# A new issue order for a hand-scheduled RG-LRU and gated-unit kernel, with one output copy on another engine

## The chip, the core and the metric

The kernel runs on one core of one Trainium2 chip. The core has five engines that run their own instruction streams: TensorE (PE in the profile, with its weight loads as PEld), VectorE (DVE), ScalarE (ACT), GpSimd (POOL) and SyncE (SP), which here issues nearly all DMA transfers. Each engine executes its instructions in the order in which they are issued; an instruction whose input isn't ready, or whose output buffer isn't free, holds all that stand behind it on that engine. The metric is device time in microseconds, median of several runs.

## What is computed

A gated linear recurrence over 6336 steps for 4 sequences of width 256, and on its output a gated linear unit whose gate is a causal convolution of 5 taps:

```python
a_base = 1.0 / (1.0 + np.exp(-a_param))
sig_r = 1.0 / (1.0 + np.exp(-r_gate))
sig_i = 1.0 / (1.0 + np.exp(-i_gate))
log_a = c * sig_r * np.log(np.clip(a_base, 1e-06, 1.0 - 1e-06))[None, None, :]
a_t = np.exp(log_a)
norm = np.sqrt(np.maximum(1.0 - a_t * a_t, 1e-06))
x_gated = norm * sig_i * x
for t in range(S):
    h = a_t[:, t] * h + x_gated[:, t]
    y[:, t] = h
...
for k in range(K):
    gate_pre += conv_w[k][None, None, :] * xp[:, k:k + S, :]
gate = 1.0 / (1.0 + np.exp(-gate_pre))
val = x @ w_val
return (gate * val @ w_out).astype(np.float32)
```

In the second half `x` is the `y` of the first. Inputs x, r_gate, i_gate and the output are float32 arrays of 26 MB each, so some 104 MB pass between memory and core.

## The kernel before

The 25344 rows (4 x 6336) are cut into 51 windows of 512 rows (the first two and the last have 256). A chunk (28 of them, line 17) is one or two windows; most work on a chunk of 1024 rows at once. Rows arrive with time along the partitions, as they lie in memory; the recurrence needs channels along the partitions and time along the free axis, so data is transposed on TensorE. The 256 channels are two halves, h = 0 and 1.

There are no loops that set the order. The text ORDER (line 38) is a list of 976 words, and lines 557 to 563 go through it and issue each word's operation. A word is a name, its indices, and behind @ the PSUM banks (of eight) that TensorE writes. Each engine's stream is what is left of the list when the other engines' words are taken out. The words, for window w, chunk c, half h:

- lr.w, li.w, lx.w: loads of r_gate, i_gate, x of a window (SP, line 292); st.w: store of the output (SP, line 546). r, i and x have rings of four windows, so a load waits until the window four before it has been used.
- ta.c, tb.c: tanh of half of r and of half of i (ACT, lines 310 and 313), which gives the sigmoids.
- tr.c.h: transposes of ta's result (TensorE, line 357); ex.c.h: a_t by Exp, out of PSUM (ACT, line 378).
- sq.c.h: a_t squared (POOL, line 386; sa on ACT, line 394); rt.b: Sqrt for a batch b of up to three chunks (ACT, line 405; batches on line 20). Sqrt needs another activation table than Tanh and Exp, so each root stands between two table loads (line 562), some roots sharing a pair.
- pp.w, up.w: 1 + tanh, and its product with x (POOL, lines 320 and 332); for windows 1, 2 and 6 TensorE passes x through PSUM (xp, line 337) and VectorE makes the product (uv, line 346).
- nt.c: the norms transposed back (TensorE, line 420); xg.c: times the product (DVE, line 450); xt.c: transposed to channels (TensorE, line 461); sc.c.h: the recurrence as a scan (DVE, line 483).
- cv.w: the convolution as 20 matmuls with diagonal weights (TensorE, line 495); tg.w: its tanh (ACT, line 502); vl.w: y times w_val (TensorE, line 510); gv.w: gate times value (DVE, line 515); ou.w: times w_out (TensorE, line 525).
- cd.w.0 or ca.w.0: copy of the output out of PSUM, on VectorE (line 533) or ScalarE (line 535), before its store.
- wm.k: five matmuls of 512 columns whose result nobody reads (TensorE, line 364).
- s_ident, s_small, s_kt, s_diag, s_wl.k, s_wcast: constants. s_kt holds a transpose on TensorE, small operations on VectorE and an Exp on ACT (line 237), and gives khf, the scale of all ex.

The last two chunks (26 and 27) take another way through nt, xg and xt (lines 428 to 446). In steady state a chunk goes through loads, ta/tb, tr, ex, sq, then waits for its batch's rt, then nt, xg, xt, sc, and its windows through cv, tg, vl, gv, ou, copy, store. The last full batch is rt.10, for chunks 23 to 25, which are windows 43 to 48; rt.11 is for chunks 26 and 27.

Of the kernel before, what the change touches and what calls it, by code (L numbers as in the profile page):

```python
# [48 lines left out]
sc.4.0 li.11 lr.15 lr.16 st.2 up.7 pp.9 li.14 li.13 vl.3@0,1 vl.4@4,5 gv.3 gv.4 cd.1.0 ou.3.0@0,1 pp.10 up.8 sq.8.1
cd.3.0 cv.6@6,7 st.1 ou.4.0@2,3 wm.12@4 tg.6 cd.4.0 wm.1@4 nt.5@2,3 xg.5 lx.10 tb.7 st.3 vl.6@0,1 gv.6 ta.9 xt.5@2,3  # L50
ou.6.0@0,1 cv.5@6,7 nt.6@4,5 ta.10 up.9 sc.5.0 sc.5.1 lx.11 up.10 wm.0@2 tr.9.0@2,3 tg.5 st.4 lx.12 tb.8 vl.5@6,7
ex.9.0 xg.6 cd.6.0 xt.6@4,5 pp.11 sq.8.0 pp.12 tr.9.1@0,1 up.11 ex.9.1 li.16 li.15 lr.19 lr.20 gv.5 lr.22 st.6 lr.21
nt.7@6,7 cv.7@2,3 sc.6.1 up.12 ou.5.0@0,1 sc.6.0 sq.9.0 tg.7 tb.9 cv.8@2,3 cd.5.0 xg.7 lx.13 lx.14 li.18 ta.11
# [540 lines left out]
```

## Time and profile before

| | us |
|---|---|
| median of 3 runs | 288.65 |
| lowest and highest | 288.52, 288.95 |
| span of the profiled execution (first to last instruction) | 286.4 |
| bytes moved by DMA | 104.76 MB, 366 GB/s on average |

The profile was taken in one execution. A row of the windows view gives, for a stretch of time, the busy time of each engine with the number of its instructions, the TensorE clock that was granted, the busy share of the 16 DMA engines and the bytes per second. A row of the timeline gives start, duration, engine, line, operation, written and read tiles with shapes, the count of merged instructions, and in brackets the idle time ahead of it with what ended it. On ACT and DVE an instruction's record overlaps the next one's by about 0.1 us, so the cost of one in a full stream is the distance from its start to the next start.

### The profile page before, as it was taken

How to read it: one execution, taken by the hardware profiler on the slowest of the kernel's cores; microseconds unless marked ns; L12 is line 12 of the kernel's file. 1: busy time of each engine (PE TensorE's matmuls, PEld its weight loads, DVE VectorE, ACT ScalarE, POOL GpSimd, SP SyncE). 2: the span in 40 equal slices, each digit the busy share in tenths (PEclk: the TensorE clock that was granted, in tenths of full speed). 3: DMA queues.
4: the chain of work that ended last, by engine and by line, in shares of the span. 5: the costliest groups of instructions: out<-in, count | busy, mean ns of one | idle time of the engine just before them, and what ended most of it. 6: DMA issues, size and time to landing. Idle time of an engine off the chain costs nothing.

```text
span 286.4 us, 6382 instructions
## 1 busy us (share of the span) xinstructions
PE 251.8 (88%) x2552; PEld 171.1 (60%) x2576; DVE 246.8 (86%) x214; ACT 273.6 (96%) x198; POOL 241.6 (84%) x161
## 2 busy tenths in 40 slices
PE   1387778899999999988988999989989899999993
PEld 1253447456656767455756676656646774767562
DVE  4002898969999899999999999999999999999991
ACT  5999999999999999999999999999999999898984
POOL 1659589899999999999999999999996999874600
PEclk9999999999999999999999999999999999999999
DMA  7999999999999999999999999999999999994536
GB/s 243 384 373 407 409 403 408 388 366 376 410 408 366 418 367 392 414 410 334 405 364 413 411 332 356 420 416 419 415 401 333 359 416 406 364 356 170 192 150 256
DMA packets 29996, 104.76 MB, mean 366 GB/s; under 512 B 3335, under 2 KB 3854, under 8 KB 29966
## 3 DMA queue, kind: packets, MB, share of 16 engines
q1 hardware_dynamic: 29952, 104.35, 94.5%
q8 instruction: 20, 0.33, 0.5%
q14 instruction: 10, 0.08, 0.1%
q10 hardware_dynamic: 14, 0.01, 0.0%
HBM read 78.39 MB, written 25.95 MB: 364 GB/s over the span
## 4 chain that ended last, share of the span: by engine, by line
ACT 33%; PE 29%; DVE 14%; issue 12%; DMA 8%; SPq 1%; ACTq 0%; DVEq 0%
ACT ering L405 8%; PE banks L495 8%; DVE yring L483 7%; PE banks L525 7%; DMA rring<-in_r_gate_dram 6%; ACT tgring L502 6%; ACT taring L310 5%; ACT tbring L313 5%; ACT aring L378 5%; PE banks L510 5%; PE banks L461 3%; DVE tgring L515 3%; PE banks L420 3%; ACT L562 3%; DVE oring L533 2%
## 5 line engine op out<-in xcount | busy, mean ns | idle before, releaser
L386 POOL TENSOR_TENSOR ering<-aring 128x1024 f32<-128x1024 f32 (+2 forms) x54 | 91.5, 1714 | 16.7 <-ACT aring L378 16.4
L332 POOL TENSOR_TENSOR uring<-tbring,xring 128x1024 bf16<-128x1024 bf16 (+1 forms) x48 | 101.1, 2119 | 3.6 <-DMA xring<-in_x_dram 3.1
L483 DVE TENSOR_TENSOR_SCAN yring<-aring,yring,banks 128x1024 bf16<-128x1024 f32 (+5 forms) x50 | 101.7, 2064 | 2.1 <-PE banks L461 1.9
L495 PE MATMUL banks<-yring,diag 64*64 64x512 bf16 (+7 forms) x1080 | 62.1, 361 | 2.3 <-ACT aring L378 1.6
L515 DVE SCALAR_TENSOR_TENSOR tgring<-tgring,banks 128x1024 bf16<-128x1024 bf16 (+1 forms) x51 | 59.1, 1178 | 4.0 <-PE banks L510 3.4
L320 POOL TENSOR_SCALAR tbring<-tbring 128x1024 bf16<-128x1024 bf16 (+1 forms) x48 | 49.1, 1032 | 6.8 <-ACT tbring L313 6.7
L378 ACT ACTIVATE aring<-banks,khf 128x2048 f32<-128x2048 bf16 (+3 forms) x38 | 54.2, 1476 | 0.4 <-PE banks L357 0.3
L525 PE MATMUL banks<-wo,tgring 128*128 128x256 bf16 x396 | 51.0, 274 | 3.7 <-DVE tgring L515 3.2
L502 ACT ACTIVATE tgring<-banks 128x1024 bf16<-128x1024 f32 (+1 forms) x51 | 50.2, 1011 | 2.0 <-PE banks L495 1.9
L510 PE MATMUL banks<-yring,wv 128*128 128x512 bf16 (+4 forms) x192 | 48.1, 359 | 3.7 <-ACT tgring L502 1.9
L310 ACT ACTIVATE taring<-rring 128x2048 bf16<-128x2048 f32 (+2 forms) x28 | 47.9, 1718 | 1.4 <-DMA rring<-in_r_gate_dram 1.4
L525 PEld LDWEIGHTS <-tgring 128*128 128x128 bf16 x396 | 41.2, 114 | 13.1 <-DVE tgring L515 8.8
L313 ACT ACTIVATE tbring<-iring 128x2048 bf16<-128x2048 f32 (+2 forms) x28 | 48.2, 1726 | 0.0
L405 ACT ACTIVATE ering<-ering 128x4096 bf16<-128x4096 f32 (+5 forms) x16 | 44.8, 2840 | 0.1
L495 PEld LDWEIGHTS <-diag 64*64 64x64 bf16 x1080 | 29.0, 106 | 25.6 <-issue 9.9
L533 DVE COPY oring<-banks 128x1024 f32<-128x1024 f32 (+1 forms) x36 | 41.9, 1182 | 1.4 <-PE banks L525 0.7
L357 PE MATMUL banks<-ident_b,taring 128*128 128x128 bf16 x396 | 29.9, 230 | 9.4 <-ACT taring L310 6.7
L357 PEld LDWEIGHTS <-taring 128*128 128x128 bf16 x396 | 26.5, 103 | 14.2 <-ACT taring L310 7.4
L510 PEld LDWEIGHTS <-wv 128*128 128x128 bf16 x216 | 19.7, 98 | 24.5 <-issue 10.3
L450 DVE TENSOR_TENSOR uring<-banks,uring 128x2048 bf16<-128x2048 bf16 (+2 forms) x26 | 29.4, 1134 | 3.5 <-PE banks L420 3.2
L420 PE MATMUL banks<-ident,ering 128*128 128x128 f32 x192 | 28.3, 289 | 1.1 <-ACT ering L405 0.9
L461 PE MATMUL banks<-ident,uring 128*128 128x128 f32 x192 | 25.9, 276 | 3.5 <-DVE uring L450 2.8
(49 smaller groups left out, 154.0 us busy)
## 6 DMA issues: line engine op xcount, KB each, us to landing
rring<-in_r_gate_dram SPq DMA_DIRECT2D x48, 512.0 KB, 8.2
iring<-in_i_gate_dram SPq DMA_DIRECT2D x48, 512.0 KB, 8.7
xring<-in_x_dram SPq DMA_DIRECT2D x48, 512.0 KB, 8.2
out_dram<-oring SPq DMA_DIRECT2D x48, 512.0 KB, 6.5
...
```

The costliest lines, as they stand in the source:

```text
L310: nc.scalar.activation(**tangent(c, taring, NTR, rring, NRI))
L313: nc.scalar.activation(**tangent(c, tbring, NTI, iring, NII))
L332: nc.gpsimd.tensor_tensor(out=u, in0=t1, in1=xt, op=ALU.mult)
L378: nc.scalar.activation(out=dst, in_=src, func=ACT.Exp, scale=khf[:, h:h + 1], bias=khf[:, h:h + 1])
L386: nc.gpsimd.tensor_tensor(out=e, in0=a, in1=a, op=ALU.mult)
L405: nc.scalar.activation(out=ering[:].bitcast(BF16)[:, 4 * o:4 * o + 2 * n], in_=ering[:, 2 * o:2 * o + 2 * n], func=ACT.Sqrt, scale=-0.25, ...
L483: nc.vector.tensor_tensor_scan(out=yring[:, h, col:col + o1 - o0], data0=aring[:, h, a_at[c] + o0:a_at[c] + o1], data1=xT[:, o0:o1], initi ...
L495: nc.tensor.matmul(out=gp[oh * 64:oh * 64 + 64, h, a:b], lhsT=diag[half * 64:half * 64 + 64, h, k, :], rhs=yring[half * 64:half * 64 + 64, ...
L502: nc.scalar.activation(out=tgring[:, w % NTG, :, 0:wins[w]], in_=live.pop(("gp", w))[:, :, 0:wins[w]], func=ACT.Tanh, scale=0.5)
L510: nc.tensor.matmul(out=val[:, m, a:b], lhsT=wv[:, hk, m * P:(m + 1) * P], rhs=yring[:, hk, col:col + b - a], start=(hk == 0), stop=(hk == ...
L515: nc.vector.scalar_tensor_tensor(out=tgring[:, w % NTG, :, 0:wins[w]], in0=tgring[:, w % NTG, :, 0:wins[w]], scalar=1.0, in1=live.pop(("va ...
L525: nc.tensor.matmul(out=ops[:, j * D:(j + 1) * D], lhsT=gv[:, hk, j:wins[w]:J], rhs=wo[:, hk, :], start=(hk == 0), stop=(hk == H - 1))
```

## The change

Only ORDER is rewritten, as a whole, together with three small things that it needs: s_kt and s_diag get their PSUM bank as an argument (they had banks 0 and 1), and op_sv, which no word called, is dropped. CHUNKS and BATCHES are the same lists with other line breaks. Both lists have 976 words. They hold the same words apart from the banks, with one exception: cd.22.0 has become ca.22.0. All rings, sizes and instructions are the same.

Of TensorE's 267 words 72 keep their place in its stream, of ACT's 53 of 177, of VectorE's 55 of 176, of POOL's 39 of 154, of SP's 26 of 210; most of the others move by a few places.

The words that the prediction speaks of, first in the start of the list (the lines of before and after are cut):

```diff
-s_ident s_small s_kt s_diag lr.2 lr.0 s_wl.3 lr.1 li.0 lr.3 s_wl.2 ta.2 ta.0 lr.4 tr.0.1@0 tr.2.0@1 lr.6 ta.1 lr.5
-tr.1.0@2 tb.0 tr.0.0@3 li.1 tr.2.1@4 ex.2.0 li.2 tr.1.1@5 li.3 ex.1.1 lx.0 ex.0.1 sq.1.1 li.4 ex.1.0 sq.2.0 ex.0.0
-ex.2.1 sq.1.0 ta.3 sq.2.1 pp.0 sq.0.0 sq.0.1 ta.4 tb.1 lr.10 tr.3.0@4,5 tb.2 lr.9 lr.8 lr.7 lx.2 tr.3.1@2,3 ex.3.0
-s_wl.1 up.0 lx.1 lx.4 wm.10@6 ex.3.1 sq.3.0 wm.5@6 lx.3 wm.3@6 tb.3 sq.3.1 wm.9@6 wm.6@6 ta.6 pp.4 sq.4.1 ta.5 lr.13
-li.5 xp.2@2,3 li.6 sq.4.0 li.7 lr.14 tr.5.0@4,5 lx.6 uv.2 pp.3 rt.0 rt.2 nt.0@0 up.4 xg.0 rt.1 xt.0@0,1 xp.1@2 rt.3
-sc.0.0 nt.1@3 up.3 lx.5 nt.2@0 uv.1 s_wl.0 xg.1 xg.2 xt.1@2,3 sc.0.1 lx.7 sc.1.0 nt.3@6,7 lr.12 sc.1.1 xg.3 ex.5.0
-xt.2@0,1 sc.2.1 sc.2.0 tb.4 cv.0@2,3 tr.5.1@4,5 xt.3@6,7 lr.11 li.8 sq.5.0 ex.5.1 tg.0 sc.3.0 pp.5 sc.3.1 cv.2@0,1
...
+s_ident wm.1@5 lr.0 lr.1 lr.2 s_small s_kt@4 li.0 ta.1 ta.0 lr.3 tr.0.1@7 tr.0.0@0 lr.4 ta.2 tr.2.0@3 tb.0 ex.0.0
+ex.2.0 ex.0.1 tr.2.1@1 ex.2.1 wm.6@4 tr.1.0@5 lr.5 lr.6 ta.3 li.1 li.2 lx.0 tr.1.1@4 wm.3@0 ex.1.1 ex.1.0 wm.5@0 ta.4
+li.4 li.3 sq.2.1 pp.0 sq.1.1 up.0 s_diag@5 lr.7 lr.9 lr.10 lr.8 tb.1 tb.2 lx.2 sq.0.0 tr.3.0@6,7 ex.3.0 s_wl.1 lx.4
+s_wl.2 lx.1 sq.1.0 sq.2.0 sq.3.0 sq.0.1 tb.3 tr.3.1@2,3 ex.3.1 sq.4.1 sq.4.0 sq.3.1 ta.6 ta.5 xp.2@4,5 uv.2 li.6 li.5
+s_wl.3 lx.3 xp.1@2 uv.1 rt.1 rt.0 nt.0@7 rt.2 xg.0 rt.3 xt.0@2,7 sc.0.0 pp.3 pp.4 up.4 nt.1@4 xg.1 nt.2@6 xg.2
+xt.1@5,2 sc.0.1 sc.1.1 up.3 xt.2@4,6 lx.6 s_wl.0 lx.5 li.8 cv.0@0,1 tg.0 lr.12 lr.13 lr.14 lr.11 tr.5.1@2,3 tb.4
+sc.1.0 sc.2.1 s_wcast sc.2.0 nt.3@0,1 ex.5.1 tr.5.0@4,5 ex.5.0 pp.5 xg.3 xt.3@0,1 sc.3.0 up.5 cv.2@6,7 tg.2 cv.1@2,3
...
```

The copy of window 22, and the load of window 45 with the tangent that reads it:

```diff
-vl.23@6,7 xt.15@4,5 ta.19 sq.18.1 sq.18.0 sq.17.0 sq.17.1 ou.24.0@2,3 tb.17 cd.22.0 gv.23 li.33 li.34 cv.26@0,1
-st.31 tb.22 xg.20 li.43 lr.48 lr.47 vl.34@0,1 vl.33@2,3 gv.34 lx.42 up.39 gv.33 st.27 xt.20@4,5 cv.35@6,7 vl.35@0,1
-ou.33.0@2,3 tg.35 cv.36@6,7 pp.42 up.40 li.44 pp.41 ta.24 sc.20.0 ca.33.0 tg.36 up.41 li.46 gv.35 tr.23.1@0,1
-nt.21@2,3 ex.23.1 sc.20.1 vl.36@6,7 xg.21 gv.36 tr.23.0@4,5 xt.21@2,3 nt.22@0,1 ta.25 ex.23.0 sq.23.1 li.45
...
+sc.14.0 pp.29 li.32 li.34 st.21 ou.22.0@0,1 ca.22.0 cv.24@6,7 vl.23@2,3 sc.14.1 tg.24 ta.20 vl.24@0,1 gv.24 st.22
+ta.24 cv.36@4,5 gv.35 ca.33.0 up.41 tg.36 sc.20.1 nt.21@0,1 lx.42 li.43 li.46 li.44 st.30 st.33 li.45 st.32 lx.44
+sq.24.0 sq.24.1 tr.25.0@4 ex.25.0 cd.34.0 nt.22@2,3 xg.22 tr.25.1@0 ou.35.0@4,5 cd.35.0 cv.37@6,7 tb.23 tb.24 sc.21.1
```

The stretch behind the last full root, rt.10:

```diff
-cv.41@0,1 st.33 gv.38 vl.37@6,7 lx.45 lr.50 st.35 cd.36.0 lx.46 ou.38.0@2,3 gv.37 li.47 rt.10 cv.40@4,5 tg.41
-ou.37.0@6,7 cd.38.0 nt.23@2,3 up.43 li.48 lr.49 st.36 cd.37.0 vl.41@6,7 xg.23 vl.40@0,1 up.45 gv.41 st.34 tg.40
-nt.24@2,3 xt.23@6,7 gv.40 up.46 xg.24 ou.39.0@0,1 cv.42@2,3 sc.23.0 ou.41.0@4,5 sc.23.1 tb.25 ca.39.0 ou.40.0@0,1
-lx.47 tg.42 vl.42@2,3 ta.27 ca.41.0 gv.42 tr.27.1@6 xt.24@4,5 ca.40.0 st.37 lx.48 li.49 tr.27.0@7 cv.43@0,1 ex.27.1
-ta.26 ex.27.0 vl.43@2,3 sc.24.0 tg.43 tb.26 pp.47 pp.48 up.47 li.50 st.39 st.38 st.41 nt.25@6,7 up.48 gv.43
-cv.44@0,1 vl.44@2,3 tg.44 xg.25 tr.26.0@4 sa.27.1 ex.26.0 ou.42.0@6,7 pp.49 lx.49 ca.42.0 xt.25@0,1 gv.44 st.40
...
+pp.44 ou.36.0@6,7 cd.36.0 tg.38 cv.39@0,1 sa.25.1 tg.39 up.44 vl.37@2,3 gv.37 vl.38@0,1 gv.38 wm.18@4 rt.10 vl.39@2,3
+up.43 sc.22.1 ou.38.0@6,7 ou.37.0@0,1 gv.39 cv.41@4,5 tg.41 lx.45 lr.49 lx.46 st.36 up.45 cd.37.0 up.46 cd.38.0
+cv.40@2,3 tg.40 nt.23@0,1 xg.23 vl.41@6,7 vl.40@4,5 gv.41 st.38 lx.48 lx.47 lx.49 nt.24@2,3 ta.27 tb.25 gv.40
+ou.39.0@0,1 xg.24 pp.48 pp.47 xt.23@6,7 sc.23.0 ou.40.0@4,5 tb.27 ca.39.0 ta.26 tr.27.1@2 ex.27.1 cv.42@0,1 ca.40.0
+sc.23.1 tg.42 vl.42@2,3 gv.42 li.49 st.40 lx.50 ou.41.0@4,5 ca.41.0 sa.27.1 up.48 pp.50 up.47 xt.24@1,0 sc.24.0
+cv.43@6,7 cv.44@4,5 vl.43@2,3 tg.43 gv.43 tg.44 nt.25@6,7 xg.25 tr.26.1@1 ex.26.1 tr.27.0@5 ex.27.0 vl.44@2,3 tb.26
...
 
-        def s_kt():
-            kps = banks[:, 0]
+        def s_kt(at):
+            kps = banks[:, at]
```

s_diag is changed in the same way.

More of the change, by code (lines that the diff above doesn't have):

```diff
@@ L49 @@
[L49 to L53, printed above, removed]
@@ L103 @@
+gv.50 ou.50.0@3 ca.50.0 st.50
 """
@@ L249, in s_kt, with s_diag @@
                                     scalar2=4.0 * math.log(1.0 - 1e-6), op0=ALU.max, op1=ALU.min)
-        def s_diag():
-            wps = banks[:, 1]
+        def s_diag(at):
+            wps = banks[:, at]
             for h in range(H):
@@ L386, in op_sq @@
             nc.gpsimd.tensor_tensor(out=e, in0=a, in1=a, op=ALU.mult)
-        def op_sv(c, h):
-            e, a = squares(c, h)
-            nc.vector.tensor_tensor(out=e, in0=a, in1=a, op=ALU.mult)
         def op_sa(c, h):
@@ L549 @@
         emit = dict(wm=op_wm, xp=op_xp, lr=op_lr, li=op_li, lx=op_lx, ta=op_ta, tb=op_tb, pp=op_pp, up=op_up, uv=op_uv, tr=op_tr, ex=op_ex,
[L550 removed]
+                    sq=op_sq, sa=op_sa, rt=op_rt, nt=op_nt, xg=op_xg, xt=op_xt, sc=op_sc, cv=op_cv, tg=op_tg,
                     vl=op_vl, gv=op_gv, ou=op_ou, cd=op_cd, ca=op_ca, st=op_st, s_small=s_small, s_ident=s_ident,
```

97 lines of the change are left out of this document (50 added, 47 removed).

## The prediction

> **What bounds the kernel now.** I read the page's busy shares first, then the busy time of each engine by stage, then ScalarE's instructions in order of time at both ends.
>
> ```profile
> PE 251.8 (88%) x2552; PEld 171.1 (60%) x2576; DVE 246.8 (86%) x214; ACT 273.6 (96%) x198; POOL 241.6 (84%) x161
> ```
>
> ScalarE (ACT) has the highest share, but a share is an average. The stages say where it is full:
>
> ```profile
> core 0 of [0], span 286.4 us
> core 0: us, PE busy (x) PEld busy (x) DVE busy (x) ACT busy (x) POOL busy (x), PEclk, DMA share, GB/s
> 0.00:20.00 20.00, 8.32 (x58) 6.24 (x59) 3.80 (x20) 16.02 (x18) 8.24 (x16) 1.00 0.92 333
> 20.00:160.00 140.00, 126.40 (x1258) 85.93 (x1272) 124.62 (x104) 139.42 (x89) 133.97 (x85) 1.00 1.01 392
> 160.00:244.20 84.20, 79.82 (x869) 53.40 (x868) 83.25 (x63) 84.04 (x56) 81.54 (x50) 1.00 1.00 390
> 244.20:287.00 42.80, 37.30 (x377) 25.55 (x382) 35.11 (x29) 34.13 (x37) 17.84 (x13) 0.98 0.65 242
> ```
>
> From 20 to 244.2 us ACT is busy for 139.42 + 84.04 = 223.46 of 224.2 us. It cannot be packed tighter there: 0.74 us is all that an order could win. VectorE (83.25 of 84.2) and the DMA engines (share 1.00) are nearly as full from 160 on, but it is ACT that never stops. The stage ends where the root rt.10 ends:
>
> ```profile
> 238.87 5.33 ACT L405 ACTIVATE ering<-ering 128x6144 bf16<-128x6144 f32 x1
> ```
>
> 244.20 us is that end; what follows hangs on it: the norms of chunks 23 to 25 are transposed (nt), multiplied in (xg), transposed again (xt), scanned (sc), convolved and projected (cv, vl, ou). There TensorE takes over: 37.30 of the last 42.8 us, of which the last 3 or so hold no instruction but the end of the last store. The waits of TensorE's matmuls in that stretch, longest first, are one entry:
>
> ```profile
> PE banks L525 <- DVE tgring L515: 0.8, 1, 0.8
> ```
>
> That one is the last window's own chain. So the tail after rt.10 is a full TensorE as well. The reader is to see three stages: a head with some ACT idling, a body that is ACT's sum and nothing else, a tail that is TensorE's sum. An order can help only in the head, or by moving work of ACT from before rt.10 to behind it, or of TensorE from behind it to before.
>
> **The change part by part.** I sorted both lists by engine and compared what stands before each root and behind it.
>
> *The copy of window 22.* One operation changes its engine: cd.22.0 (VectorE) becomes ca.22.0 (ACT); ACT has 16 output copies in place of 15. A copy of that size on ACT, and the start of the instruction behind it:
>
> ```profile
> 220.30 1.02 ACT L535 COPY oring<-banks 128x1024 f32<-128x1024 f32 x1
> 221.19 1.05 ACT L502 ACTIVATE tgring<-banks 128x1024 bf16<-128x1024 f32 x1
> ```
>
> Start to start it is 221.19 - 220.30 = 0.89 us. It stands near 160 us, in the full stretch, before rt.8, so rt.8 to rt.10 all come **0.9 us** later. Apart from it ACT's set of operations before rt.10 is the same in both lists, also the 18 table loads, and its set behind rt.10 too: nothing else was moved across. VectorE is spared one copy, but xg.23 waits for rt.10, not for VectorE; that relief is worth nothing on this path. Bounds: 0.16 (all of the stage's idle 84.2 - 84.04 swallowed) less, so 0.7, to 0.9.
>
> *The head.* ACT's instructions before the first roots, with their waits:
>
> ```profile
> 3.85 0.20 ACT L237 ACTIVATE ktmp<-ktmp 128x2 f32<-128x2 f32 x1 [1.85 <-DVE ktmp L236]
> 4.54 1.58 ACT L310 ACTIVATE taring<-rring 128x1024 bf16<-128x1024 f32 x2 [0.49 <-DMA rring<-in_r_gate_dram]
> 6.35 0.63 ACT L310 ACTIVATE taring<-rring 128x512 bf16<-128x512 f32 x1 [0.23 <-DMA rring<-in_r_gate_dram]
> ...
> 8.63 2.60 ACT L378 ACTIVATE aring<-banks,khf 128x256 f32<-128x256 bf16 x5 [0.29 <-PE banks L357]
> 11.10 1.93 ACT L310 ACTIVATE taring<-rring 128x2048 bf16<-128x2048 f32 x1
> 13.40 1.91 ACT L310 ACTIVATE taring<-rring 128x2048 bf16<-128x2048 f32 x1 [0.38 <-DMA rring<-in_r_gate_dram]
> ...
> 24.55 1.91 ACT L310 ACTIVATE taring<-rring 128x2048 bf16<-128x2048 f32 x1 [0.28 <-DMA rring<-in_r_gate_dram]
> ...
> 33.39 1.28 ACT L562 ACT_TABLE_LOAD   x1
> ```
>
> Behind the first tangent the idle is 0.23 + 0.29 + 0.38 + 0.28 = 1.18 us; the 0.49 before it is 1.67 in all. The new load order starts with the small windows 0 and 1 and puts two weight loads of 64 KB (s_wl.2, s_wl.3) behind; at 390 GB/s that is 0.34 us for all loads behind them, most of the 0.38. The four loads lr.7 to lr.10 leave as one block today,
>
> ```profile
> 15.34 1.75 SPq L292 DMA_DIRECT2D rring<-in_r_gate_dram  x4
> ```
>
> when the tangent of 13.40 has ended (15.31), because lr.10 stands first; lr.7 needs only the slot that the tangent of 11.10 frees at 13.03, and in the new list it stands first, so the 0.28 goes too. Against this, five filler matmuls (wm.1) now run ahead of s_kt's transpose on TensorE, and ACT's Exp of s_kt stands ahead of the first tangent. At the head's pace (below: 0.114 us for 128 columns, so 0.46 for 512) they take 2.3 us, mostly under the wait for a_param; I let 0.7 us stick out, so Exp at 4.55 and the first tangent at 4.8 instead of 4.54. Sum: +0.25 - 0.34 - 0.28, and about 0.1 for khf, which comes 0.7 later too: **-0.3 us**; bounds -1.7 (every wait gone) to +0.5.
>
> *The first conv gate.* Behind the table load of 33.39 ACT now calls tg.0 first (ex.5.0 before). tg.0 needs cv.0, cv.0 the scans of chunk 0. TensorE's rows there:
>
> ```profile
> 15.37 2.74 PE L357 MATMUL banks<-ident_b,taring 128*128 128x128 bf16 x24 [1.25 <-ACT taring L310]
> 17.90 6.31 PE L364 MATMUL banks<-ident_b 128*128 128x512 bf16 x25
> 25.90 1.95 PE L337 MATMUL banks<-xring,ident 128*128 128x512 f32 x4 [1.69 <-DMA xring<-in_x_dram]
> ...
> 27.69 1.06 PE L357 MATMUL banks<-ident_b,taring 128*128 128x128 bf16 x16
> ...
> 35.02 0.74 PE L495 MATMUL banks<-yring,diag 64*64 64x256 bf16 x20
> ```
>
> cv.0 ends at 35.76 today; ACT will ask for it at 33.39 + 1.28 = 34.7. Today nt.3 stands ahead of cv.0 on TensorE, and nt.3 waits for rt.3, which ends at 33.39; the new order puts nt.3 behind cv.0, but uv.1, with the late window 1, ahead of the first xg on VectorE. I expect cv.0 to end between 34 and 35: **+0.2 us**, bounds 0 and 1.1 (35.76 - 34.67) if TensorE keeps its pace. Whether it does is the first rival.
>
> *The body.* With 0.74 us of idle nothing can be gained but much can be lost. I took for every ACT instruction the time between its producer's end and its own start in this trace, and corrected it by how much more or less work the two lists put ahead of either. All producers on TensorE and POOL stay on time by this (the narrowest is rt.4, which loses almost all of its 3 us). The loads are closer. The narrowest is li.45, for the tangent tb.24:
>
> ```profile
> 218.37 2.34 SPq L292 DMA_DIRECT2D iring<-in_i_gate_dram  x3
> ```
>
> ```profile
> 233.62 1.98 ACT L313 ACTIVATE tbring<-iring 128x2048 bf16<-128x2048 f32 x1
> ```
>
> ```profile
> iring<-in_i_gate_dram SPq DMA_DIRECT2D x48, 512.0 KB, 8.7
> ```
>
> The third of these issues (li.45) leaves at about 219.3 and lands some 9 us later, 228.5, for 233.62: 5 us spare. In the new list three more transfers of 512 KB stand ahead of it (3 x 1.34 us at 390 GB/s = 4.0), one of them a store that waits for its copy, and tb.24 is called 2.3 us sooner. 5.1 - 4.0 - 2.3 = -1.2 us: ACT would wait that long once. Since everything ahead may shift alike I take **+0.3 us**, bounds 0 and 1.3.
>
> *The tail.* Both lists hold the same operations behind nt.23 on TensorE and behind xg.23 on VectorE. The order differs at one place that matters: TensorE ran cv.43, vl.43, nt.25, cv.44; now it runs cv.43, cv.44, vl.43, nt.25.
>
> ```profile
> 256.50 1.04 PE L510 MATMUL banks<-yring,wv 128*128 128x512 bf16 x4
> 257.38 1.11 PE L420 MATMUL banks<-ident,ering 128*128 128x128 f32 x8
> 258.42 1.27 PE L495 MATMUL banks<-yring,diag 64*64 64x512 bf16 x20
> ```
>
> ```profile
> 255.79 2.34 DVE L483 TENSOR_TENSOR_SCAN yring<-aring,yring,banks 128x1024 bf16<-128x1024 f32 x1
> 258.05 1.19 DVE L515 SCALAR_TENSOR_TENSOR tgring<-tgring,banks 128x1024 bf16<-128x1024 bf16 x1
> 259.16 1.21 DVE L450 TENSOR_TENSOR uring<-banks,uring 128x2048 bf16<-128x2048 bf16 x1
> 260.81 1.22 DVE L515 SCALAR_TENSOR_TENSOR tgring<-tgring,banks 128x1024 bf16<-128x1024 bf16 x1 [0.43 <-ACT tgring L502]
> ```
>
> gv.43 (258.05) follows its scan with no wait because vl.43 has ended at 257.54. One convolution later (1.27) vl.43 ends at 258.8, and VectorE idles 0.7 us; xg.25, the scans of chunk 25 and the last windows queue behind it. Against it the 0.43 before gv.44 may go, as cv.44 and its gate are earlier. **+0.5 us**; bounds -0.4 and +1.2.
>
> Sum: 0.9 - 0.3 + 0.2 + 0.3 + 0.5 = +1.6 us. The profiled execution's span is 286.4 us; the median of the runs is 288.65, 2.25 more, which lies around the span and which the change does not touch. So the span goes to 288.0 and the time to **290.25 us**.
>
> **The rivals.**
>
> *TensorE slow at the first roots.* 24 transposes of 128 columns take 2.74 us at 15.37 (0.114 each), 16 take 1.06 at 27.69 (0.066), though PEclk shows 1.00 throughout: in the head TensorE works at about half its pace until the 25 fillers of 17.90. These fillers now stand earlier (wm.6, wm.3, wm.5 around 8 to 13 us), and between the transposes of about 16 us and lx.2's arrival TensorE would idle some 8 us. If it is slow again at 25.90, the four passes take 3.9 us instead of 1.95, the other two 1 us more; cv.0 then ends near 37, tg.0 holds ACT for about 2 us instead of 0.2: **292.0 us**. For it: the old pace in the rows. Against: nothing in this trace shows a warm TensorE turning slow, since it never idles long after 25.9. [...]
>
> *Loads late.* li.45 costs its full 1.2, and others with under 1 us left by the same working (li.19, li.22, lr.28, lr.44) 0.5 each: 290.25 - 0.3 + 1.2 + about 1 = **292.2 us**. For it: DMA share 1.00 in the whole body, so a load that slips is not made up. Against: reordering also brings other loads forward.
>
> *The head fills up, the tail holds.* The place is ACT's first 27 us: the new load order removes all waits, 1.67 us, from the first tangent on; the other terms are nothing but the copy: 288.65 + 0.9 - 1.67 = **287.9 us**. It decides from the point where the head wins more than the 0.9 of the copy. For it: three of its five waits are for loads whose order was changed. Against: the Exp of s_kt now comes later, not sooner. Half of it gives 288.7, no change.
>
> *Not what it says.* The engine of one copy is the only change of work; were ca.22.0 hidden, +0.7 remains of my sum: 289.4, inside the range of the forecast.
>
> **How the numbers follow.** A measurement of this kernel tells about 0.2% (0.58 us) from no change: below 288.07 is faster, above 289.23 slower. Forecast 0.48 (own range 289.2 to 291.4, the bounds of the terms taken half each), TensorE slow 0.15, loads late 0.13, head full 0.20, of which 0.08 faster and 0.12 no change; 0.04 for something worse, beyond 293. Of the forecast itself 0.04 falls within 0.2%. Faster 0.08, same 0.16, slower 0.76. The range runs from 288.2, between the two ends of the third rival, to 292.9, past the first two.
>
> **What would show it.** Right: ACT still over 99% busy from 35 us to the end of rt.10; rt.10 ending 0.5 to 2 us after 244.20; from there to the end of the span (286.4 - 244.2 = 42.2 us today) as long or longer; a VectorE wait for TensorE near gv.43. Head: first tangent near 4.8, no waits for rring after it. First rival: L337's four passes over 3 us and an ACT wait at L502 near 35 us. Loads: an ACT wait at L313 near 232 us. It would be wrong if rt.10 ended before 244 us, which needs ACT instructions to become shorter or its head to win over 0.9 us, or if the tail came out over 0.7 us shorter than today.

## The result, and the profile after

| | before | after |
|---|---|---|
| median, us | 288.58 (288.0 to 288.95) | 298.43 (296.71 to 299.62) |
| span of the profiled execution, us | 286.4 | 295.2 |

The changed kernel takes 1.035 times as long (95% interval 1.0303 to 1.0399): 9.85 us more, where 1.6 were forecast. Its executions lie within 2.9 us, those of before within 1. The profiled one took 297.3 us, one of the quicker. Medians here and below are over all runs; the ratios, each against runs of the kernel before from the same round, leave out runs over 1.5% above the fastest of their kernel, and where the two disagree (e13: median 298.45, ratio 1.0333 of 287.76, which is 297.3) the ratio counts.

The busy shares and the stages of the kernel after, the last two cut at its rt.10:

```profile
PE 254.5 (86%) x2576; PEld 170.5 (58%) x2576; DVE 246.4 (83%) x213; ACT 275.0 (93%) x199; POOL 242.1 (82%) x161
```

```profile
core 0: us, PE busy (x) PEld busy (x) DVE busy (x) ACT busy (x) POOL busy (x), PEclk, DMA share, GB/s
0.00:20.00 20.00, 11.65 (x71) 6.14 (x71) 3.90 (x20) 15.96 (x18) 7.45 (x15) 0.97 0.91 335
20.00:160.00 140.00, 121.37 (x1214) 82.53 (x1215) 121.09 (x98) 135.53 (x87) 131.80 (x83) 0.97 0.99 379
160.00:251.80 91.80, 83.09 (x907) 56.09 (x909) 85.77 (x67) 89.05 (x59) 84.77 (x52) 1.00 0.98 376
251.80:296.00 44.20, 38.39 (x393) 25.74 (x382) 35.62 (x30) 34.50 (x37) 18.06 (x13) 0.99 0.63 238
```

ACT's work is nearly the same (275.0 against 273.6 us), but from 20 us to the end of rt.10 it now idles 4.47 + 2.75 = 7.22 us instead of 0.74. The waits view says for whom (times in us: total, number, longest):

```profile
ACT taring L309 <- DMA rring<-in_r_gate_dram: 3.5, 4, 2.5
ACT tbring L312 <- DMA iring<-in_i_gate_dram: 3.5, 3, 1.9
```

and the timeline of ACT where:

```profile
99.31 1.91 ACT L312 ACTIVATE tbring<-iring 128x2048 bf16<-128x2048 f32 x1 [1.93 <-DMA iring<-in_i_gate_dram]
...
113.12 1.91 ACT L309 ACTIVATE taring<-rring 128x2048 bf16<-128x2048 f32 x1 [0.33 <-DMA rring<-in_r_gate_dram]
...
117.61 1.91 ACT L312 ACTIVATE tbring<-iring 128x2048 bf16<-128x2048 f32 x1 [0.62 <-DMA iring<-in_i_gate_dram]
...
159.50 1.91 ACT L312 ACTIVATE tbring<-iring 128x2048 bf16<-128x2048 f32 x1 [0.95 <-DMA iring<-in_i_gate_dram]
...
165.21 1.01 ACT L530 COPY oring<-banks 128x1024 f32<-128x1024 f32 x1
...
169.64 1.91 ACT L309 ACTIVATE taring<-rring 128x2048 bf16<-128x2048 f32 x1 [2.50 <-DMA rring<-in_r_gate_dram]
```

These are tb.11, ta.15, tb.12, tb.16, the moved copy ca.22 and ta.20. The ends of the roots, subtracted from those of before, give the same sum by stage: -0.6 us at rt.3, -0.1 at rt.5, +3.1 at rt.6 (1.93 + 0.33 + 0.62 = 2.88 of it in the first three rows), +3.0 at rt.7, +7.4 at rt.8 (0.95 + 2.50 and 0.9 for the copy, 4.35), +7.6 at rt.10, +8.8 at the last copy. Nearly all is lost in two places, and both are waits for loads.

How a load comes to be late is read from SP's timeline:

```profile
125.51 0.47 SPq L291 DMA_DIRECT2D iring<-in_i_gate_dram  x1
133.95 0.81 SPq L291 DMA_DIRECT2D rring<-in_r_gate_dram  x2
...
146.37 0.90 SPq L291 DMA_DIRECT2D xring<-in_x_dram  x2
...
148.85 0.33 SPq L291 DMA_DIRECT2D rring<-in_r_gate_dram  x1
154.79 0.34 SPq L541 DMA_DIRECT2D out_dram<-oring  x1
156.70 0.33 SPq L291 DMA_DIRECT2D xring<-in_x_dram  x1
...
159.18 1.65 SPq L291 DMA_DIRECT2D rring<-in_r_gate_dram  x2
```

From 125.51 SP issues nothing for 8.4 us: next in its list is lr.33, whose slot ta.16 frees at 133.9. Behind it stand two x loads and two stores (lx.25, lx.26, st.14, st.15) whose buffers are free by 130. The DMA engines run dry meanwhile (last two columns: share, GB/s):

```profile
120.00:130.00 10.00, 8.70 (x76) 5.16 (x79) 8.17 (x8) 9.94 (x6) 10.00 (x7) 1.00 1.03 417
130.00:140.00 10.00, 9.73 (x101) 6.69 (x90) 9.72 (x8) 10.00 (x8) 9.37 (x6) 1.00 0.78 268
```

lx.25, behind st.17 and lr.37, for which SP stands until 143.5 and 146.0, leaves at 146.4, 16 us after its slot was free, so POOL's product of window 25 is late, so the slot of lx.29 is (156.70). lr.38, behind st.20 (SP stands for it until 154.79) and lx.29 in the list, is issued at 159.18 though its slot was free at 146.0; it lands at 169.6 for ta.20, which ACT could have begun at 169.64 - 2.50 = 167.1. Whether the late issue or the 10.4 us to the landing is to blame is tested below (e10, e11).

At the other place no unready buffer blocks SP. li.19, for tb.11, leaves at 89.3, behind li.20, st.7, lx.15 and lr.26, 5 us after its slot is free, and lands at 99.2; the slot that tb.11 writes waits for POOL's product of window 15, and this for lx.15 (86.4 to 96.7), which was moved back as well.

```profile
87.65 0.33 SPq L291 DMA_DIRECT2D rring<-in_r_gate_dram  x1
89.26 0.33 SPq L291 DMA_DIRECT2D iring<-in_i_gate_dram  x1
```

The second row is li.19. It leaves when lx.16, eight places ahead of it in SP's list, has landed (89.24); st.7, lx.15 and lr.26 wait in the same way (0.2, 0.9 and 0.9 us, li.19 1.3). In the traces of before and after no issue of SP starts before the transfer eight places ahead has landed, wherever that landing is recorded (151 and 152 issues), and in after SP waits 40 us, in 52 places, for landings (30 us in 37 before). By estimate a place farther back then costs the time of one transfer, some 1.3 us: 512 KB at the 392 GB/s of before's body.

POOL shows the x loads' lateness most (idle time of the group, and of it for x loads; 3.1 us before):

```profile
L331 POOL TENSOR_TENSOR uring<-tbring,xring 128x1024 bf16<-128x1024 bf16 (+1 forms) x48 | 101.0, 2117 | 12.5 <-DMA xring<-in_x_dram 10.9
```

The head and the first conv gate, TensorE first:

```profile
24.62 4.93 PE L336 MATMUL banks<-xring,ident 128*128 128x512 f32 x6 [8.00 <-DMA xring<-in_x_dram]
```

```profile
20.00:30.00 10.00, 5.15 (x8) 2.09 (x8) 1.89 (x3) 9.97 (x9) 9.11 (x8) 0.56 1.04 379
```

```profile
4.63 0.20 ACT L236 ACTIVATE ktmp<-ktmp 128x2 f32<-128x2 f32 x1 [2.64 <-DVE ktmp L235]
...
34.07 0.60 ACT L497 ACTIVATE tgring<-banks 128x512 bf16<-128x512 f32 x1
```

TensorE idles 8.00 us, is granted 0.56 of its clock, and the six passes take 4.93 us against 1.95 + 1.02 = 2.97 before. In this execution ACT still doesn't wait for it at tg.0.

### The profile page after: what moved, and what is told of

The parts are those of the page before. It is cut to its first block, busy times and chain, and to the rows that moved or that the text cites. A ratio compares the mean times of both kernels' runs of the same rounds, so it can differ in the third digit from the quotient of the medians.

```text
span 295.2 us, 6403 instructions
## 1 busy us (share of the span) xinstructions
PE 254.5 (86%) x2576; PEld 170.5 (58%) x2576; DVE 246.4 (83%) x213; ACT 275.0 (93%) x199; POOL 242.1 (82%) x161
## 4 chain that ended last, share of the span: by engine, by line
DMA 24%; PE 21%; ACT 18%; POOL 13%; DVE 11%; issue 11%; SPq 1%; ACTq 0%; DVEq 0%; POOLq 0%
DMA iring<-in_i_gate_dram 10%; PE banks L490 6%; DMA xring<-in_x_dram 6%; DMA rring<-in_r_gate_dram 6%; POOL ering L385 5%; ACT taring L309 5%; POOL uring L331 5%; DVE yring L478 4%; PE banks L520 4%; ACT aring L377 4%; PE banks L505 4%; DVE tgring L510 3%; ACT tbring L312 3%; ACT tgring L497 2%; PE banks L336 2%
## 5 line engine op out<-in xcount | busy, mean ns | idle before, releaser
L385 POOL TENSOR_TENSOR ering<-aring 128x1024 f32<-128x1024 f32 (+2 forms) x54 | 91.5, 1713 | 11.7 <-ACT aring L377 11.5
L510 DVE SCALAR_TENSOR_TENSOR tgring<-tgring,banks 128x1024 bf16<-128x1024 bf16 (+1 forms) x51 | 59.1, 1181 | 11.4 <-PE banks L505 7.0
L490 PE MATMUL banks<-yring,diag 64*64 64x512 bf16 (+7 forms) x1080 | 61.4, 361 | 1.1 <-ACT aring L377 0.9
L520 PE MATMUL banks<-wo,tgring 128*128 128x256 bf16 x396 | 50.3, 273 | 7.2 <-DVE tgring L510 3.5
L505 PE MATMUL banks<-yring,wv 128*128 128x512 bf16 (+4 forms) x216 | 49.2, 361 | 3.4 <-ACT tgring L497 2.0
L520 PEld LDWEIGHTS <-tgring 128*128 128x128 bf16 x396 | 42.0, 114 | 15.4 <-DVE tgring L510 7.4
L309 ACT ACTIVATE taring<-rring 128x2048 bf16<-128x2048 f32 (+2 forms) x28 | 47.3, 1713 | 3.6 <-DMA rring<-in_r_gate_dram 3.5
L528 DVE COPY oring<-banks 128x1024 f32<-128x1024 f32 (+1 forms) x35 | 40.7, 1185 | 1.9 <-PE banks L520 1.2
L505 PEld LDWEIGHTS <-wv 128*128 128x128 bf16 x216 | 19.5, 97 | 26.6 <-issue 11.5
L445 DVE TENSOR_TENSOR uring<-banks,uring 128x2048 bf16<-128x2048 bf16 (+2 forms) x26 | 29.4, 1133 | 5.6 <-PE banks L415 2.9
L356 PE MATMUL banks<-ident_b,taring 128*128 128x128 bf16 x396 | 28.6, 223 | 6.2 <-ACT taring L309 3.5
L356 PEld LDWEIGHTS <-taring 128*128 128x128 bf16 x396 | 25.1, 100 | 11.5 <-issue 5.3
```

Source lines behind the costliest of these rows:

```text
L309: nc.scalar.activation(**tangent(c, taring, NTR, rring, NRI))
L356: nc.tensor.transpose(out=bank[:, o:o + P], in_=taring[:, place(w, NTR), j, h * P:(h + 1) * P], identity=ident_b[:])
L385: nc.gpsimd.tensor_tensor(out=e, in0=a, in1=a, op=ALU.mult)
L490: nc.tensor.matmul(out=gp[oh * 64:oh * 64 + 64, h, a:b], lhsT=diag[half * 64:half * 64 + 64, h, k, :], rhs=yring[half * 64:half * 64 + 64, ...
L505: nc.tensor.matmul(out=val[:, m, a:b], lhsT=wv[:, hk, m * P:(m + 1) * P], rhs=yring[:, hk, col:col + b - a], start=(hk == 0), stop=(hk == ...
L510: nc.vector.scalar_tensor_tensor(out=tgring[:, w % NTG, :, 0:wins[w]], in0=tgring[:, w % NTG, :, 0:wins[w]], scalar=1.0, in1=live.pop(("va ...
```

## The experiments

Lag behind the kernel before, in us, of the ends of some roots and of the last copy in the profiled execution, with medians of all runs. "After" and "before" in the first column say which kernel was edited. A single profiled execution of a kernel with the new head lies up to 2 us off its median, so stages are compared by differences along a row.

| run | rt.3 | rt.5 | rt.6 | rt.7 | rt.8 | rt.10 | end | median | ratio, 95% |
|---|---|---|---|---|---|---|---|---|---|
| after | -0.6 | -0.1 | 3.1 | 3.0 | 7.4 | 7.6 | 8.8 | 298.43 | 1.0351 [1.0303, 1.0399] |
| e1, after | 3.5 | 8.8 | 19.8 | 20.8 | 29.4 | 32.5 | 42.3 | 329.45 | 1.1429 [1.138, 1.1478] |
| e2, before | 1.1 | 11.4 | 17.0 | 25.4 | 30.4 | 41.6 | 44.7 | 336.59 | 1.1729 [1.1655, 1.1803] |
| e3, after | 0.7 | 0.8 | 3.4 | 3.3 | 5.4 | 6.2 | 6.7 | 297.23 | 1.0328 [1.0277, 1.038] |
| e4, before | 0.4 | 0.4 | 0.5 | 0.4 | 2.0 | 2.0 | 2.0 | 289.92 | 1.0076 [1.0061, 1.0091] |
| e5, after | 0.4 | 1.5 | 4.6 | 4.5 | 9.8 | 10.2 | 10.7 | 298.97 | 1.0377 [1.0349, 1.0404] |
| e6, both | 1.1 | 2.4 | 6.6 | 8.9 | 8.8 | 8.8 | 8.8 | 296.58 | 1.0294 [1.026, 1.0328] |
| e7, both | -0.2 | -0.2 | -0.2 | -0.3 | 3.8 | 4.4 | 5.1 | 293.82 | 1.0218 [1.0179, 1.0256] |
| e8, after | 0.4 | 1.3 | 4.7 | 4.6 | 11.3 | 11.5 | 12.0 | 299.60 | 1.0347 [1.0311, 1.0384] |
| e9, after | 1.4 | 1.8 | 2.9 | 2.8 | 5.4 | 6.5 | 7.0 | 297.64 | 1.0346 [1.0315, 1.0376] |
| e10, after | 0.5 | 1.5 | 3.5 | 3.5 | 4.3 | 5.0 | 5.6 | 295.43 | 1.0249 [1.0209, 1.0288] |
| e11, after | 0.9 | 2.3 | 5.3 | 5.2 | 6.4 | 9.7 | 10.2 | 298.67 | 1.0358 [1.032, 1.0395] |
| e12, after | 0.6 | 1.1 | 3.1 | 3.0 | 3.8 | 5.2 | 6.2 | 294.82 | 1.0232 [1.0205, 1.0259] |
| e13, after | 0.4 | 1.4 | 4.0 | 3.9 | 5.9 | 7.4 | 7.9 | 298.45 | 1.0333 [1.0291, 1.0375] |
| e14, after | 1.7 | 3.1 | 4.8 | 4.7 | 5.4 | 7.5 | 8.0 | 294.70 | 1.0237 [1.0192, 1.0282] |
| e15, after | 1.8 | 3.0 | 4.7 | 4.6 | 5.6 | 7.2 | 7.9 | 296.29 | 1.0284 [1.026, 1.0308] |
| e16, both | 0.7 | 4.0 | 4.0 | 4.0 | 4.0 | 4.0 | 4.0 | 292.07 | 1.0129 [1.0102, 1.0155] |
| e17, both | -0.8 | 1.5 | 3.5 | 3.4 | 4.2 | 5.1 | 5.8 | 294.23 | 1.0213 [1.019, 1.0237] |
| e18, before | -0.6 | -0.6 | -0.6 | -0.5 | -0.6 | -0.6 | -0.6 | 288.24 | 1.0018 [0.9998, 1.0038] |

**Whole lists exchanged.** e1 is the kernel after with SP's list of before, e2 the kernel before with SP's list of after; the compute engines' orders stay.

```diff
-SP's words in the order of the one list
+SP's words in the order of the other
```

> The changed kernel with one engine's list put back: SyncE's (all loads, stores and weight loads) has the order of the kernel before; TensorE, VectorE, ScalarE and GpSimd keep the new order. Theory (late loads): the 6.3 us that ScalarE waits for loads between 90 and 170 us (0.33 + 1.93 + 0.62 + 0.95 + 2.50) go nearly all, rt.10 ends near 245 to 246 us instead of 251.8, and the time falls from 298.4 to 291 to 293 us. Rival (the order of the compute engines, the copy on ScalarE and TensorE's half pace at 25 us are the cause): 296 us or more.

> The kernel before with only SyncE's list taken from the change. Theory (late loads): ScalarE, which never waited for a load after 25 us, now waits for several, and the time rises from 288.6 by 3 us or more, to 292 to 297 us. Rival (compute order): within 1 us of 288.6.

Both are far slower than the kernels they were made from, by 31 and 49 us, and both theories fall. The new list of loads is not bad in itself: each list fits its own compute order, and the pairing counts. In e2 the waits are those of late gate loads,

```profile
ACT tbring L311 <- DMA iring<-in_i_gate_dram: 21.9, 5, 7.7
ACT taring L308 <- DMA rring<-in_r_gate_dram: 17.7, 6, 5.2
```

and in e1 ACT's roots wait most, 17.2 us for POOL's squares. A whole exchange adds more mismatch than it removes, so these two could not tell the theories apart.

**The copy.**

```diff
# e3, in after
-ca.22.0
+cd.22.0
# e4, in before
-cd.22.0
+ca.22.0
```

> The changed kernel with the copy of window 22 back on VectorE. By the prediction's term the time falls by 0.9 us. By the trace of the change the copy stands at 165.2 us, ahead of a 2.50 us wait of ScalarE for a load at 169.6, so that taking it away only makes this wait longer: within 0.4 us of the changed kernel (298.4).

> The kernel before with the copy of window 22 on ScalarE. ScalarE is full there, so by its sum the time rises by 0.9 us, to 289.5 (0.3%). If something else set the pace at 165 us: 288.6, no change.

In the kernel before the copy costs 289.92 - 287.60 = 2.3 us and not 0.9. It waits for its matmul and holds ACT meanwhile:

```profile
170.53 1.01 ACT L533 COPY oring<-banks 128x1024 f32<-128x1024 f32 x1 [0.55 <-PE banks L523]
```

The table shows 1.6 of it between rt.7 and rt.8 and 0.4 in the head, which is chance. In the kernel after, taking it back wins 1.2 us by the medians, less than their spread, so these runs don't show a gain: there the copy runs right ahead of ta.20's wait, which would cover it.

**Fillers and clock.** e5 puts the new order's early wm words back behind the transposes of about 16 us.

```diff
# TensorE: wm.10, wm.5, wm.3, wm.9, wm.6 behind tr.3.1, wm.1 behind wm.12
```

> The changed kernel with its fillers wm.10, wm.5, wm.3, wm.9 and wm.6 behind tr.3.1 on TensorE, as in the kernel before, and wm.1 behind wm.12. Theory: the granted clock's dip to 0.56 between 20 and 30 us goes, the six passes at L336 take about 3.0 us instead of 4.93, ScalarE's Exp of s_kt comes at 3.9 instead of 4.6; as ScalarE did not wait at tg.0 the time changes by under 1 us from 298.4, but the runs, which fell in two groups (296.7 to 297.3 at a mean clock of 0.983, 299.6 at 0.971), come closer together. If TensorE's slow start is the cause of the loss: 292 us or less.

The six passes of window 1 and 2 now take 1.98 + 1.10 us, tg.0 has no wait, and the time doesn't fall. The slow clock is real (0.56 from 20 to 30 us in after, 1.00 in e5), but it isn't where the time goes.

**Halves.** e6 runs the new order for 438 words (to about 132 us) and then the old, e7 the old and then the new.

```diff
# e6: words 1 to 438 of after, then the others in the order of before
# e7: words 1 to 438 of before, then the others in the order of after
```

> Spliced: the new list up to its word 438 (ta.16, about 132 us), and behind it all other words in the order of the kernel before (the two prefixes differ by four words there). Theory (loads late at several places, each lost for good since ScalarE is full): it keeps the lag that the change has at rt.6, 3.1 us, and gains no more: 290.5 to 292.5 us. Rival (the loss is at one place behind, or in the tail): 288 to 289 us.

> The other splice: the old list up to word 438 (ta.16), and behind it the new order. Theory: the waits for loads before 132 us (2.9 us) go, those of 159.5 and 169.6 us (3.4 us) may stay, the tail's 1.2 us stays: 292 to 295 us. If the late loads at 159 to 170 us were a consequence of transfer time lost before 132 us: 289 to 291 us.

Both halves lose, and the sum (8.6 + 5.8) is over after's 9.9, as a seam, the place where the two lists meet, costs too (2.2 us from rt.6 to rt.7 in e6). In e7 nothing is lost up to rt.7, and yet this wait stands:

```profile
166.02 1.91 ACT L308 ACTIVATE taring<-rring 128x2048 bf16<-128x2048 f32 x1 [2.66 <-DMA rring<-in_r_gate_dram]
```

So the second place isn't a consequence of the first.

**Loads moved one by one.** All in SP's list of after.

```diff
# e8: li.19 alone, as in e9
# e9
 st.6
+lx.15
 lr.24 lx.16 st.2 lr.23 st.5
+li.19
 li.20 st.7
-lx.15
 lr.26
-li.19
# e10
 st.13 li.26
+st.14 st.15 lx.26 lx.25
 lr.33 lr.34 li.27
-st.14
 li.28 lx.28 st.16 lx.27 st.17 lr.37
-lx.25 lx.26 st.15
# e11
 lr.36
+lr.38 li.31
 st.20 lx.29
-li.31
 st.18 lx.30
-lr.38
# e12: e9, e10 and e11
```

> The changed kernel with one load moved in SyncE's list: li.19 ahead of li.20 (it stood four transfers behind it). Theory: ScalarE's wait of 1.93 us at 99.3 us (tb.11) goes, and with it the lag that it gave: 296 to 297 us. If the later waits merely grow by as much: 298 us.

> The kernel after, with two loads forward in SP's list: lx.15 ahead of lr.24, li.19 ahead of li.20. Theory (a load that stands behind a blocked or less urgent one on SP's list costs its wait): tb.11 had two late inputs, li.19 itself and the gate product of window 11, whose ring slot is free only when the x load of window 15 has been used. With both forward the 1.93 us wait at tb.11 goes, the tangent roots of batch 6 to 8 lag the kernel before by about 5.4 instead of 7.4 us, and the time is about 296.4. Rival (DMA is full there, so moving loads forward only changes who waits): the wait comes back at another load before 120 us and the time stays at 298 to 299.

> The kernel after, with st.14, st.15, lx.26 and lx.25, whose buffers are free by 130 us, put ahead of lr.33, for which SP stands blocked until ta.16 ends at 133.9. Theory (the DMA engines ran dry behind the blocked lr.33): the DMA share from 130 to 140 us rises from 0.78 to 0.95 or more, the waits at tb.16 (0.95) and ta.20 (2.50) shrink by some 2 us together, and the time is about 296.4. Rival (the 8 us block is harmless, the loads behind it are late for their own places in the list): the share rises, the two waits stay within 0.5 us of what they were, 298 to 299.

> The kernel after, with lr.38 and li.31 ahead of st.20, on which SP stands blocked from 148.9 to 154.8 us. Theory: lr.38 lands some 8 us earlier, the 2.50 us wait at ta.20 goes or falls under 0.5 (another load takes the rest), the lag behind the kernel before grows by 2 us less between the roots of batch 7 and 8, about 296.2. Rival (DMA is full): lx.29 or lx.30 or another gate load is late in its place and the time stays at 298 to 299.

> The kernel after with the three edits of the SP list of the runs before together. Theory: the waits of 1.93, 0.33, 0.95 and 2.50 us go, some 5 of the 7.6 us that the body lost, and the time is 293 to 294. Rival (DMA is full and order alone can't pay): under 1.5 us gained, 297 or more.

With li.19 alone forward (e8), tb.11 waits as long as before, for its other late input, the slot that POOL frees once lx.15 is there:

```profile
100.99 1.91 ACT L311 ACTIVATE tbring<-iring 128x2048 bf16<-128x2048 f32 x1 [2.18 <-POOL uring L330]
```

With both (e9) that wait is gone and from rt.5 to rt.6 1.1 us are lost instead of 3.2. In the table this stretch costs 2.0 to 4.2 us in the eight kernels with the new body that leave lx.15 in its place (after, e3, e5, e6, e8, e10, e11, e13) and 1.1 to 2.0 in the five that move it (e9, e12, e14, e15, e17). But the median falls only 0.8 us and the ratio not at all (1.0346), so that this is won in time isn't shown. e10 decides the second place: share and rate stay up, and lr.38, issued at the same time as in after (159.12 against 159.18), is there for ta.20 at 166.50, where after waited until 169.64.

```profile
130.00:140.00 10.00, 9.73 (x101) 6.48 (x94) 9.73 (x8) 10.00 (x8) 9.32 (x7) 1.00 1.03 416
```

```profile
159.12 1.76 SPq L290 DMA_DIRECT2D rring<-in_r_gate_dram  x2
```

```profile
166.50 1.93 ACT L308 ACTIVATE taring<-rring 128x2048 bf16<-128x2048 f32 x1
```

So the chain by way of lx.25, POOL and lx.29 is not what cost the time: lr.38 leaves no sooner. It lands sooner: in after it took 10.4 us with seven transfers in flight ahead of it, in e10 at most 7.4, as ta.20 starts there without a wait. 10.4 us for eight transfers, lr.38 among them, are 1.3 each, and at that 7.4 us are six at most: by this estimate some of those that the dry spell had pushed back no longer stand in its way. The loss from rt.7 to rt.8 goes from 4.4 to 0.8 us, the median down by 3.0 (2.9 by the ratios), and the ratio's interval lies clear of after's. One profile would prove little, as this loss varies, but the table holds: 2.0 to 6.7 us in the seven kernels with the new order of loads there (after, e3, e5, e7, e8, e9, e13), 0.7 to 1.2 in the six with the edit of e10 or e11 (these two, e12, e14, e15, e17). e11 mends the same wait from the other side (lr.38 leaves 7 us earlier; 1.2 us lost from rt.7 to rt.8) but no time is won: SP's next block is longer (7.3 us ahead of lx.40, 4.6 in after), and 2 us go in its profile at a gate that waits for TensorE, with the DMA share at 0.71 from 200 to 210 us:

```profile
206.64 1.02 ACT L496 ACTIVATE tgring<-banks 128x1024 bf16<-128x1024 f32 x1 [1.96 <-PE banks L489]
```

All three together (e12) give back 3.6 us (3.4 by the ratios), against 5 expected: one wait comes back elsewhere.

```profile
113.81 1.91 ACT L308 ACTIVATE taring<-rring 128x2048 bf16<-128x2048 f32 x1 [1.76 <-DMA rring<-in_r_gate_dram]
```

That is ta.15. Its loads can only leave at the end of ta.13 (two chunks of r fill the ring). From there to the start of ta.15 the kernel before has 11.9 us, all of them work; after has 6.8 with 0.33 of waiting, e12 8.3 with 1.76.

**What is left.** e13 and e14 move words of ACT, e15 takes the copy back in e14, e16 and e17 join heads and bodies at word 150, near 45 us.

```diff
# e13, ACT in after
-ta.3
 ex.1.1 ex.1.0
+ta.3
# e14: e12 and e13; tb.12 ahead of ta.15 on ACT, li.22 ahead of lx.19 on SP
# e15: e14 with
-ca.22.0
+cd.22.0
# e16: words 1 to 150 of e13, then the others as in before
# e17: words 1 to 150 of before, then the others as in e12
```

> The kernel after, with ta.3 behind the two Exps of ex.1 instead of ahead of them. Theory: in the runs of the new head so far ta.3 waited 0.4 to 2.0 us for its load, and the roots of batch 0 ended 0.1 us early to 1.9 us late; 1.0 us of other work ahead of ta.3 hides up to 1.0 us of that wait. The median falls by 0.5 to 1.0, to about 297.6. Rival (the spread of the new order's times has another source): no change, 298.4.

> The kernel with three edits of SP's list (294.8) and two on ScalarE: ta.3 behind ex.1, and tb.12 ahead of ta.15 (with li.22 ahead of lx.19). Theory: ta.15 can't be fed in time because its ring slots come free at the end of ta.13, 8.3 us ahead of its start; with tb.12 (1.9 us) between, its wait of 1.76 goes, and with the head's 0.5 to 1.0 the time is about 292.3. Rival (the wait passes to tb.12 or the next): 294 to 295.

> The kernel of the run before this with the copy of window 22 back on VectorE. Theory: with the wait at ta.20 gone, nothing hides the copy (1.0 us on ScalarE and what it waits for TensorE; 2.3 us when it was put into the kernel before): 1 to 2 us less than the run before, about 290.8. Rival (VectorE is as full as ScalarE, the copy costs the same there): no change.

> The new order's first 150 words (to about 45 us, with ta.3 behind ex.1), then the order before. Theory: the new head is worth 0.3 to 0.6 us less the spread of its loads, and the old body keeps that: 287.5 to 288.2 against 287.9. Rival (what stands in flight at the seam doesn't fit the old body's loads): over 289.

> The order before for its first 150 words (to about 45 us), then the new order with the three edits of SP's list. Theory: the new head costs 1 us on average (late first loads) and gives the spread of 2 us between executions; without it the time falls from 294.8 to about 293.6, its runs within 1 us of each other. Rival (the head is not the cause): 294.5 or more, or the spread stays.

e13 can't be told from after, and e14 not from e12. In e13's profile the tangents ahead of and behind ta.3 wait instead (0.56 and 0.26 us, and 0.63 at ex.1); in e14's the wait at ta.15 has become one of the gates behind it, for TensorE:

```profile
120.96 2.10 ACT L496 ACTIVATE tgring<-banks 128x1024 bf16<-128x1024 f32 x2 [1.37 <-PE banks L489]
```

In e15 the copy's way back wins nothing; two gates behind it wait 0.39 (for VectorE) and 0.59 us instead. e16 loses all its 4.0 us before rt.5 and not one tenth after: the old body, begun 4 us late, doesn't care. Of the 4.0, 2.3 are the seam, where fillers of both heads meet in front of a transpose that ACT needs:

```profile
48.40 2.32 PE L362 MATMUL banks<-ident_b 128*128 128x512 bf16 x10
50.56 1.06 PE L355 MATMUL banks<-ident_b,taring 128*128 128x128 bf16 x16
```

```profile
51.66 4.01 ACT L376 ACTIVATE aring<-banks,khf 128x2048 f32<-128x2048 bf16 x2 [2.26 <-PE banks L355]
```

The new head itself so costs some 1.7 us there. e17, with the same seam (2.33), has four runs within 0.6 us of each other, where e12's spread over 2.4. That this spread comes from the new head isn't shown: e7, with the old head, spreads over 2.6, and e15, with the new one, over 0.3. The gain expected from leaving that head out is eaten by the seam. Behind its seam the mended body loses another 5.8 - 1.5 = 4.3 us, and e17's trace says where: ACT waits for the loads of ta.15 (1.66), ta.23 (0.30) and tb.24 (0.52), the copy adds 0.9 to its work (182.72 us from rt.4 to rt.10, 181.79 before), and the tail takes 0.7; that is 4.1.

```profile
114.09 1.92 ACT L308 ACTIVATE taring<-rring 128x2048 bf16<-128x2048 f32 x1 [1.66 <-DMA rring<-in_r_gate_dram]
235.95 1.91 ACT L311 ACTIVATE tbring<-iring 128x2048 bf16<-128x2048 f32 x1 [0.52 <-DMA iring<-in_i_gate_dram]
```

No version beats the kernel before.

**One block in the kernel before.**

```diff
# e18, SP in before
 lx.23 lx.24
+lr.33
 st.15 st.13 li.27 li.28 lr.34
-lr.33
```

> The kernel before with one load moved: lr.33, whose slot comes free at the end of ta.16 (130.9 us), ahead of st.15, st.13, li.27 and li.28. SP then stands blocked from 123.3 to 130.9 instead of issuing these at 126 to 129.5. Theory: the DMA engines run dry for some 2 us between 130 and 135 us, the loads behind come 2 us later, and where the old list leaves under 2 us (tb.15, li.28 3.3 us early; tb.16, li.29 3.2 us) a wait of up to 1.5 us appears: 288.3 to 289.3 against 287.8. Rival (the loads in flight cover the block): 287.8, DMA share near 1.0 in every slice.

From 122.75 SP stands for 7.5 us, and the DMA engines run dry by more than in after,

```profile
122.37 0.80 SPq L290 DMA_DIRECT2D xring<-in_x_dram  x2
130.27 0.33 SPq L290 DMA_DIRECT2D rring<-in_r_gate_dram  x1
```

```profile
120.00:130.00 10.00, 9.20 (x70) 5.74 (x70) 9.71 (x8) 9.97 (x5) 10.00 (x6) 1.00 0.78 309
130.00:140.00 10.00, 8.48 (x100) 6.78 (x103) 9.91 (x8) 10.00 (x8) 10.00 (x8) 1.00 0.85 303
```

so far as the theory said; but no wait appears, the lag is the same at all roots, and no loss can be told from no change (ratio 1.0018, 0.9998 to 1.0038). In the old list the loads behind the block have that much slack. This block alone costs nothing; in after one of about the same length meets loads without slack.

## Why the prediction was wrong

- **The bound** was right: ACT is the sum of the body, and every microsecond that it waits shows at the end (the waits at the two places and the copy, 7.2 us, against a lag that grows by 7.7 from rt.5 to rt.10).
- **The body is the step that failed:** "Since everything ahead may shift alike I take +0.3 us, bounds 0 and 1.3." Copy and body together were put at 1.2 us and measured 7.6 + 0.1 = 7.7 between rt.5 and rt.10. The working took each load's landing from the trace of before and corrected it for transfers moved ahead of it. It did not replay SP: an issue that isn't ready, for its buffer (lr.33, 8.4 us) or for the landing eight places ahead (li.19, 1.3 us), holds all behind it, so the new list makes its own issue times. And it looked at loads that ACT reads, not at x loads, whose lateness reaches ACT by way of POOL (tb.11 in e8). The load that it called the narrowest, li.45, was on time in after, with 0.5 us to spare (landed 237.77, tb.24 from 238.27); in eight of the other kernels tb.24 does wait for it, 0.3 to 1.2 us. Of the four others that it named under the rivals, three were late (li.19 for tb.11, lr.28 for ta.15, li.22 for tb.12). e10 shows that the order of SP alone makes most of the second place, 3.0 us of the time. That the order of loads makes the first is read from the traces of e8 and e9, and no run shows it in time.
- **The rival "loads late"** had the mechanism and three of the places, at 292.2: 0.5 us for each where tb.11 alone took 1.93, and the place of 2.50 was not among them.
- **The copy** was put at 0.9. In e4 it cost 2.3, with 0.55 of waiting for its matmul that "start to start" leaves out; in the changed kernel e3 and e15 show no gain that can be told from their spread. The term was too small where it was tested alone; in the mended body of e17 the copy adds the 0.9 to ACT's work, but taking it away (e15) only lets ACT wait elsewhere.
- **The head**, -0.3: the Exp at 4.63 (4.55 forecast) and rt.3 at -0.6 look right in the profile shown, but that execution was a lucky one. In 13 profiled executions with the new head rt.3 lags by -0.6 to +1.8, mean +0.8; in five with the old one by -0.8 to +0.4. The step that assumed the loads to land as they did before fails here too.
- **tg.0**, +0.2 with bounds 0 and 1.1: no wait in after, 0.46 to 0.98 us in eight others with the new head (e6, e8, e10, e11, e13 to e16). **The rival "TensorE slow"** was right in what it described (8.00 us idle, 0.56 of the clock from 20 to 30 us) and wrong in its price of 2 us: 0 to 1. In after's trace the last matmul ahead of the idling ends at 16.61; the granted clock is 1.00 until 18 us, 0.50 from 19 to 28 and 1.00 again from 29.
- **The tail**, +0.5 with an upper bound of 1.2, measured +1.2, but not for the cause given: gv.43 waits 0.20 us, and for ACT's tangent, not for vl.43. Most of it is the product of chunk 24, which waits for POOL, and POOL for lx.46. In eleven other kernels with this tail it costs 0.5 to 0.7, the size forecast, in five of them with 0.4 to 0.5 us at gv.43, again for the tangent: there the size and the place were right, and the cause was not.

```profile
255.69 2.18 POOL L331 TENSOR_TENSOR uring<-tbring,xring 128x1024 bf16<-128x1024 bf16 x1 [1.41 <-DMA xring<-in_x_dram]
```

```profile
257.90 1.23 DVE L445 TENSOR_TENSOR uring<-banks,uring 128x2048 bf16<-128x2048 bf16 x1 [0.89 <-POOL uring L331]
...
267.25 1.22 DVE L510 SCALAR_TENSOR_TENSOR tgring<-tgring,banks 128x1024 bf16<-128x1024 bf16 x1 [0.20 <-ACT tgring L497]
```

Of the 9.85 us, SP's three edits give back 3.6 (e12 against after), the new head costs about 1.7 (e16 without its seam), and 4.3 stay in the body after those edits (e17 behind its seam): 9.6, roughly, as medians and single profiles are mixed here, and as e12 against e17 would put the head nearer 2.9 (0.5 between their losses, and the seam). Why rt.3 comes up to 2.4 us apart in the profiles with the new head, and what it would take to feed ta.15, ta.23 and tb.24 in time, stays open.
